# Weights by casting GpSimd DMAs, one staging buffer each for Q, K and V, and the attention's norm in four pieces

## The chip, the cores and the metric

The kernel runs on one core of one Trainium2 chip. The metric is the device time in microseconds (us); lower is better. Executions of one kernel agree to within about 1%. The profile shows one execution: its *span* is the time from its first to its last instruction, and beside it stands the *granted clock* of TensorE, where 1.00 is full speed.

Engines: TensorE (PE) multiplies matrices, VectorE (DVE), ScalarE (ACT) and GpSimd (POOL) do the rest, SyncE (SP) issues transfers. The transfers themselves are made by DMA engines, 16 by the profile's count.

## The reference

Linear attention with an RMS norm, then a two-layer network with ELU.

```python
kv  = einsum('bhsd,bhse->bhde', k, v)             # 8 batches, 8 heads, 576 tokens, head width 64
out = einsum('bhsd,bhde->bhse', q, kv)
rms = sqrt(mean(out * out, axis=-1, keepdims=True) + 1e-6)
a   = out / rms * g_norm
x   = a.transpose(0, 2, 1, 3).reshape(4608, 512)  # 4608 tokens, 512 wide
h   = x @ w_in                                    # 512 x 2048
g   = where(h > 0, h, exp(min(h, 0)) - 1)
y   = g @ w_out                                   # 2048 x 512, float32
```

All inputs are float32. The kernel multiplies in bf16, so every input is cast once.

## The kernel before

The tokens are cut into nine tiles of 512. For each tile there is attention (K'V, transposed Q, their product, the norm, a transposition to x), a *first product* of eight steps (x times w_in, with ELU), and an *output product* (times w_out). Attention for tile T+1 is woven between the steps of tile T's first product, so that TensorE has work while ScalarE and VectorE do the norm and the ELU.

Inputs come through one DMA queue, SyncE's, into a pool of six float32 staging tiles that Q, K, V and the weights share; GpSimd then casts them. (Cuts are marked `# ...`.)

```python
stage = tile_pool(name="stage", bufs=6)
# ...
def fetch_w_out(s):                       # 1 MiB of float32; fetch_w_in is alike
    st = stage_tile()[:, 0:2048]
    nc.sync.dma_start(out=st..., in_=moe_w_out...[:, 4 * s : 4 * s + 4, :])
    raw["wo", s] = st
def cast_w_out(s, eng):
    st = raw.pop(("wo", s))...
    for c in range(KC):
        copy_on(eng, w_out_sb[:, 4 * s + c, :], st[:, c, :])
# ...
def se(h):                                # half a tile of attention's product and its norm
    def run():
        se_ps = at_tile(FP32)...          # PSUM, one buffer
        for c in range(2):
            se_mm(T, 2 * h + c, st["qT"], se_ps[:, c, :])      # TensorE
        ss = sum_heads(square(se_ps, 2), 2)                    # ScalarE, then VectorE
        inv_rms(ss)                                            # ScalarE: Ln, Exp
        # ...
        scale_rows(st["xs"][:, 2 * h : 2 * h + 2, :], se_ps, ss, 2)   # VectorE
    return run
# ...
def mm1(T, i, cols=(slice(0, 512),), relu=False):   # a step of the first product
    # ... 8 matmuls into h_ps (two buffers) ...
    nc.scalar.activation(e, h_ps, AF.Exp)
    # ... with relu=True also a Relu on ScalarE ...
    def rest():                                      # VectorE: min(e,1)-1, then max (or add) into gT
        # ...
    return rest
# ... the order of loads and casts, after tile 0's attention:
for s in range(2): cast_w_in(s, Q)        # fetched right behind tile 0's Q, K and V
fetch(1)                                  # Q, K, V of tile 1
cast_all(1)
for s in range(2, 4): fetch_w_in(s)
for s in range(2, 4): cast_w_in(s, Q)
for s in range(4): fetch_w_out(s); cast_w_out(s, Q)
fetch(2)
at = attention(1)
steps = {2: "q", 3: "kv", 4: "se0", 6: "se1"}
for i in range(8):                        # first product of tile 0
    # ...
    mm1(0, i, cols, relu=(i % 2 == 1))()
    if i in steps: at[steps[i]]()
mm2_half(0, 0); mm2_half(0, 1)            # first output row block of tile 0: needs all of w_out
at["x"]()                                 # transposition of tile 1
mm2_half(0, 2)
cast_all(2); fetch(3)
# ... tile 1 and the later tiles
```

In the traces an instruction that waits holds up those behind it on its engine (ScalarE's Exp stood 2.48 us behind a waiting Ln), and the loads of one DMA queue landed in the order of their issue.

Of the kernel before, what the change touches and what calls it, by code (L numbers as in the profile page):

```python
# [8 lines left out]
FP32 = mybir.dt.float32  # L9
# [7 lines left out]
def kernel(  # L17
# [14 lines left out]
    P = 128  # L32
# [10 lines left out]
    NT = B + 1  # L43

    const = ctx.enter_context(tc.tile_pool(name="const", bufs=1))
    stage = ctx.enter_context(tc.tile_pool(name="stage", bufs=6))
    qkvp = ctx.enter_context(tc.tile_pool(name="qkvp", bufs=2))
    attp = ctx.enter_context(tc.tile_pool(name="attp", bufs=2))
    mlpg = ctx.enter_context(tc.tile_pool(name="mlpg", bufs=2))
# [19 lines left out]
    w_out_sb = const.tile([P, FC, DM], BF16, name="w_out_sb")  # L69


    def stage_tile():
        return stage.tile([P, 2304], FP32, name="st", tag="st")

    raw, bf = {}, {}

    def fetch_q(b):

        st = stage_tile()[:, 0:2048]
        raw["q", b] = st  # L80
        if b < B:
            for s in range(2):
                nc.sync.dma_start(
                    out=st.rearrange("p (s h x) -> p s h x", s=2, h=4)[:, s],
                    in_=q[b].rearrange("(h s) r d -> s h r d", s=2)[s, :, 0:G, :].rearrange(
                        "h (p j) d -> p h (j d)", j=J
                    ),
                )
        else:
            sv = st.rearrange("p (i s h d) -> p i s h d", i=J, s=2, h=4)  # L90
            for t in range(B):
                for s in range(2):
                    nc.sync.dma_start(
                        out=sv[(t % 2) * 64 : (t % 2) * 64 + 64, t // 2, s],
                        in_=q[t].rearrange("(h s) r d -> s h r d", s=2)[
                            s, :, G:S, :
                        ].rearrange("h p d -> p h d"),
                    )

    def fetch_kv(name, src, b):  # L100

        st = stage_tile()
        raw[name, b] = st
        return st.rearrange("p (h x) -> p h x", h=4), src[b].rearrange(
            "h r d -> (h r d)"
        ).rearrange("(h p x) -> p h x", h=4, p=P)
# [4 lines left out]
            out_, in_ = fetch_kv(name, src, b)  # L111
            nc.sync.dma_start(out=out_, in_=in_)

    def fetch_w_in(s):
        st = stage_tile()[:, 0:2048]
        nc.sync.dma_start(
            out=st.rearrange("p (c f) -> p c f", c=KC),
            in_=moe_w_in.rearrange("(c p) f -> p c f", p=P)[:, :, s * 512 : s * 512 + 512],
        )
        raw["wi", s] = st  # L120

    def fetch_w_out(s):
        st = stage_tile()[:, 0:2048]
        nc.sync.dma_start(
            out=st.rearrange("p (c f) -> p c f", c=KC),
            in_=moe_w_out.rearrange("(c p) f -> p c f", p=P)[:, 4 * s : 4 * s + 4, :],
        )
        raw["wo", s] = st

    def copy_on(eng, out_, in_):  # L130
        if eng is nc.scalar:
# [20 lines left out]
    def cast_kv(name, b, eng):  # L152
        sv = kv_tile(name, b)
        for lo, hi in ((0, 2), (2, 4), (4, 6), (6, 8), (8, 9)):
            copy_on(eng, bf[name, b][:, lo:hi], sv[:, lo:hi])

    def cast_w_in(s, eng):
        st = raw.pop(("wi", s)).rearrange("p (c f) -> p c f", c=KC)
        for c in range(KC):
            copy_on(eng, w_in_sb[:, c, s * 512 : s * 512 + 512], st[:, c, :])  # L160

    def cast_w_out(s, eng):
        st = raw.pop(("wo", s)).rearrange("p (c f) -> p c f", c=KC)
        for c in range(KC):
            copy_on(eng, w_out_sb[:, 4 * s + c, :], st[:, c, :])


    xT = {}
# [73 lines left out]
    def attention(T):  # L242
        st = {}

        def kv():
            if T == B:
                return
            kv_ps = at_tile(FP32)
            for u in range(2):
                kv_mm(T, [kv_ps[:, 0:512], kv_ps[:, 512:1024]], u)  # L250
            kv_v = kv_ps.rearrange("p (s x e) -> p s x e", s=2, e=P)[:, :, 0:2, :]
            bd_v = bd_kv[:, T].rearrange("p (s u) e -> p s u e", s=2)
            for l in range(2):
                ls = slice(l * 64, l * 64 + 64)
                nc.scalar.copy(bd_v[ls, :, :, ls], kv_v[ls, :, :, ls])

        def q_t():
            qt_ps = at_tile(BF16).rearrange("p (r t) -> p r t", r=NPAIR)
            for p in range(NPAIR):
                q_t_mm(bf["q", T], qt_ps, p)  # L260
            qT = attp.tile([P, NPAIR, G], BF16, name="qT", tag="qT")
            st["qT"] = qT
            nc.vector.tensor_copy(out=qT[:, 0:2, :], in_=qt_ps[:, 0:2, :])  # L263
            nc.scalar.copy(qT[:, 2:4, :], qt_ps[:, 2:4, :])  # L264

        def se(h):
            def run():
                se_ps = at_tile(FP32).rearrange("p (c f) -> p c f", c=2)
                for c in range(2):
                    se_mm(T, 2 * h + c, st["qT"], se_ps[:, c, :])  # L270
                ss = sum_heads(square(se_ps, 2), 2)
                inv_rms(ss)
                if h == 0:
                    st["xs"] = attp.tile([P, J, DM], BF16, name="xs", tag="xs")
                scale_rows(st["xs"][:, 2 * h : 2 * h + 2, :], se_ps, ss, 2)

            return run

        def x_t():
            xs = st["xs"]  # L280
            xt_ps = at_tile(BF16).rearrange("p (r t) -> p r t", r=NPAIR)
            for c in range(KC):
                for j in range(J):
                    nc.tensor.transpose(  # L284
                        xt_ps[:, c, j * P : j * P + P],
                        xs[:, j, c * P : c * P + P],
                        ident,
                    )
            x = attp.tile([P, KC, G], BF16, name="xT", tag="xT")
            xT[T] = x  # L290
            nc.vector.tensor_scalar(  # L291
                out=x[:, 0:2, :], in0=xt_ps[:, 0:2, :], scalar1=g_col, scalar2=None, op0=ALU.mult
            )
            nc.scalar.mul(x[:, 2:4, :], xt_ps[:, 2:4, :], g_col)  # L294

        return {"kv": kv, "q": q_t, "se0": se(0), "se1": se(1), "x": x_t}


    gT = {}
# [90 lines left out]
    g_src = bass.AP(tensor=g_norm.tensor, offset=g_norm.offset, ap=[[1, 64], [1, 1]])  # L390
    for i in range(2):
        nc.sync.dma_start(out=g_col[i * 64 : i * 64 + 64, :], in_=g_src)
    for s in range(2):
        fetch_w_in(s)

    q_st = q_tile(0)
    qt_ps = ps_m1.tile([P, 2, G], FP32, name="qt_ps", tag="mm1").rearrange(
# [17 lines left out]
    kv_ps = [ps_m2.tile([P, DM], FP32, name="kv_ps", tag="mm2") for _ in range(2)]  # L415
    for u in range(2):
        for n, name in enumerate("kv"):
            for eng, js in ((V, slice(0, 5)), (A, slice(5, 9))):
                copy_on(
                    eng,  # L420
                    bf[name, 0][:, js, 2 * u : 2 * u + 2, :],
                    kv_st[n][:, js, 2 * u : 2 * u + 2, :],
                )
            if (u, n) == (0, 0):
                nc.vector.tensor_copy(out=qT0[:, 0:2, :], in_=qt_ps[:, 0:2, :])
                nc.scalar.copy(qT0[:, 2:4, :], qt_ps[:, 2:4, :])
        kv_mm(0, kv_ps, u)
        if u == 0:
            idle(6)
        for eng, l in ((V, 0), (A, 1)):  # L430
            ls = slice(l * 64, l * 64 + 64)
            for s in range(2):
                copy_on(
                    eng,
                    bd_kv[ls, 0, 2 * s + u, ls],
                    kv_ps[s][ls, u * P + l * 64 : u * P + l * 64 + 64],
                )
# [57 lines left out]
    def cast_all(b):  # L495
        cast_q(b, Q)
        if b < B:
            cast_kv("k", b, Q)
            cast_kv("v", b, Q)

    for s in range(2):
        cast_w_in(s, Q)
    fetch(1)
    cast_all(1)
    for s in range(2, 4):
        fetch_w_in(s)
    for s in range(2, 4):
        cast_w_in(s, Q)
    for s in range(4):
        fetch_w_out(s)  # L510
        cast_w_out(s, Q)
    fetch(2)
    at = attention(1)
    steps = {2: "q", 3: "kv", 4: "se0", 6: "se1"}
    for i in range(8):
        cols = (slice(0, 256), slice(256, 512)) if i == 0 else (slice(0, 512),)
        mm1(0, i, cols, relu=(i % 2 == 1))()
        if i in steps:
            at[steps[i]]()
    mm2_half(0, 0)  # L520
    mm2_half(0, 1)
    at["x"]()
# [2 lines left out]
    cast_all(2)  # L525
    fetch(3)
    at = attention(2)
    halves = {0: 3, 2: 4, 4: 5, 6: 6}
    steps = {1: "q", 2: "kv", 3: "se0", 5: "se1", 7: "x"}
    for i in range(8):  # L530
        rest = mm1(1, i)
        if i in halves:
            mm2_half(0, halves[i])
        rest()
        if i in steps:
            at[steps[i]]()
    mm2_half(0, 7)

    steps = {0: "kv", 1: "q", 2: "se0", 4: "se1", 6: "x"}
    for T in range(2, NT):  # L540
        if T + 1 < NT:
            at = attention(T + 1)
            cast_all(T + 1)
        if T + 2 < B:
            fetch(T + 2)
        elif T + 2 == B:
            fetch_q(B)
        for i in range(8):
            rest = mm1(T, i)
            mm2_half(T - 1, i)  # L550
            rest()
            if T + 1 < NT and i in steps:
                at[steps[i]]()
    for i in range(8):
        mm2_half(NT - 1, i)

# [29 lines left out]
```

## Time and profile before

| | before |
|---|---|
| time, median | 323.12 us (322.09 to 323.97) |
| span of the profiled execution | 320.4 us, granted clock 1.00 |
| first product of tile 0 starts / ends (first output matmul) | 22.0 / 45.5 us |
| transposition of tile 1 / its first product start | 51.95 / 54.57 us |
| one later tile | 31.5 us |

The busy time in windows, kernel before. The columns are the window, its length, busy us and count of instructions of TensorE (PE), its weight loads, VectorE, ScalarE, GpSimd, then the clock, the DMA share and GB/s.

```profile
22.00:30.00 8.00, 6.54 (x53) 4.23 (x52) 3.71 (x5) 3.97 (x4) 6.24 (x11) 1.00 1.05 390
30.00:38.00 8.00, 5.56 (x63) 3.16 (x62) 4.09 (x6) 4.57 (x8) 7.85 (x14) 1.00 1.06 387
38.00:46.00 8.00, 5.74 (x32) 2.71 (x31) 6.75 (x8) 5.02 (x7) 7.58 (x12) 1.00 1.06 373
46.00:54.60 8.60, 5.71 (x39) 2.91 (x39) 5.06 (x6) 3.70 (x6) 7.17 (x14) 1.00 1.06 378
...
151.80:183.30 31.50, 31.29 (x212) 16.10 (x214) 19.22 (x23) 15.84 (x22) 7.90 (x14) 1.00 0.41 143
```

In a later tile (last line) TensorE is busy 31.29 of 31.50 us: nothing is to be won there. Between 22 and 54.6 us it is busy 5.6 to 6.5 of each 8 us, while the DMA engines run at 373 to 390 GB/s without a pause.

The timeline of TensorE, kernel before: start, duration, instruction, count, and in brackets the idle time before it and what ended it. L344 is the output product, L284 the transposition of tile 1, L310 the first product.

```profile
51.51 0.60 PE L344 MATMUL o_ps<-w_out_sb,gT 128*128 128x512 bf16 x2 [2.84 <-DVE gT L328]
51.95 1.06 PE L284 MATMUL at<-ident,xs 128*128 128x128 bf16 x16
...
54.57 1.89 PE L310 MATMUL h_ps<-xT,w_in_sb 128*128 128x512 bf16 x8
```

The last two matmuls of tile 0's first output block waited 2.84 us for the last ELU step (gT).

Waits, kernel before: who waited for whom, total us, times, longest.

```profile
ACT ss L231 <- DVE ss L225: 24.7, 16, 2.5
```

ScalarE stood in its queue before Ln, 16 times, for VectorE's sum; the next Exp of the ELU stood behind it. This wait is what the norm's split aims at.

The timeline of GpSimd, kernel before, the casts of w_out:

```profile
37.39 4.78 POOL L134 CAST w_out_sb<-st 128x512 bf16<-128x512 f32 x8
42.59 5.37 POOL L134 CAST w_out_sb<-st 128x512 bf16<-128x512 f32 x8 [0.42 <-DMA st<-in_moe_w_out_dram]
```

w_out is complete in bf16 at 47.96 us.

### The profile page before, as it was taken

What the parts mean: (1) busy time and instruction counts of PE and PEld (TensorE: products, weight loads), DVE (VectorE), ACT (ScalarE), POOL (GpSimd) and SP (SyncE); (2) the same over time, 40 slices, a digit from 0 to 9 for tenths busy, and PEclk for the clock granted to TensorE, in tenths of its full rate; (3) what the DMA queues carried; (4) which work ended last, traced back from release to release, by engine and by line L of the source; (5) the groups of instructions that cost most, each with busy time, mean ns of one, the idle gap of its engine ahead of it and who ended that gap; (6) DMA issues with size and microseconds to landing.
All of it is one profiled execution on the core that took longest, in us unless ns stands there. A gap on an engine that the chain in (4) does not pass through costs nothing.

```text
span 320.4 us, 4746 instructions
## 1 busy us (share of the span) xinstructions
PE 295.8 (92%) x1905; PEld 149.7 (47%) x1941; DVE 179.2 (56%) x215; ACT 151.8 (47%) x215; POOL 78.4 (24%) x140
## 2 busy tenths in 40 slices
PE   8777686988899999999999999999999999999993
PEld 3443343554454445455545455545454545444441
DVE  3466584558447754775377537744874576454400
ACT  3654654356445544544544455444544545443220
POOL 0069998920026002600260045002000000000000
PEclk9999999999999999999999999999999999999999
DMA  7999999800193019302920392024201010101122
GB/s 255 354 376 389 386 374 376 314 0 2 61 354 119 25 68 349 139 4 89 368 102 2 108 363 88 0 90 99 78 1 65 2 65 2 65 0 65 68 65 65
DMA packets 28565, 46.44 MB, mean 145 GB/s; under 512 B 5504, under 2 KB 13696, under 8 KB 28544
## 3 DMA queue, kind: packets, MB, share of 16 engines
q1 hardware_dynamic: 28544, 46.14, 41.1%
q8 instruction: 15, 0.25, 0.3%
q14 instruction: 6, 0.05, 0.0%
HBM read 36.70 MB, written 9.44 MB: 144 GB/s over the span
## 4 chain that ended last, share of the span: by engine, by line
PE 78%; DMA 7%; DVE 5%; ACT 5%; issue 2%; SPq 1%; POOL 0%; DVEq 0%
PE o_ps L344 36%; PE h_ps L310 33%; DMA st<-in_moe_w_in_dram 5%; DMA st<-in_v_dram 3%; ACT elu_e L318 2%; PE at L179 2%; PE at L284 2%; DVE gT L328 2%; PE at L189 2%; PE at L201 2%; DVE ss L225 1%; DVE elu_e L325 1%; ACT sq L220 1%; DVE xs L235 1%; ACT elu_h L322 1%
## 5 line engine op out<-in xcount | busy, mean ns | idle before, releaser
L310 PE MATMUL h_ps<-xT,w_in_sb 128*128 128x512 bf16 (+1 forms) x564 | 133.8, 376 | 6.3 <-DVE gT L328 3.6
L344 PE MATMUL o_ps<-w_out_sb,gT 128*128 128x512 bf16 x562 | 133.9, 379 | 3.6 <-DVE gT L328 2.8
L318 ACT ACTIVATE elu_e<-h_ps 128x1024 bf16<-128x1024 f32 x72 | 73.5, 1020 | 50.2 <-PE h_ps L310 49.0
L344 PEld LDWEIGHTS <-gT 128*128 128x128 bf16 x576 | 56.2, 98 | 70.6 <-DVE gT L328 3.3
L328 DVE TENSOR_TENSOR gT<-elu_e,h_ps 128x1024 bf16<-128x1024 bf16 x68 | 83.0, 1221 | 7.1
L310 PEld LDWEIGHTS <-w_in_sb 128*128 128x128 bf16 x584 | 55.2, 98 | 65.2 <-issue 3.2
L325 DVE TENSOR_SCALAR elu_e<-elu_e 128x1024 bf16<-128x1024 bf16 x72 | 33.3, 462 | 87.8 <-ACT elu_e L318 87.8
L134 POOL CAST q_bf<-st 128x512 bf16<-128x512 f32 x32 | 18.9, 629 | 125.1 <-DMA st<-in_q_dram 103.4
L354 ACT COPY o_sb<-o_ps 128x512 f32<-128x512 f32 x36 | 21.0, 583 | 24.5 <-PE o_ps L344 24.5
L235 DVE TENSOR_TENSOR xs<-at,ss 128x1024 bf16<-128x1024 f32 x16 | 19.6, 1225 | 9.9 <-ACT ss L232 9.9
L220 ACT ACTIVATE sq<-at 128x1024 bf16<-128x1024 f32 (+1 forms) x18 | 17.5, 977 | 14.5 <-PE at L201 12.0
L225 DVE TENSOR_REDUCE ss<-sq 128x16 f32<-128x1024 bf16 x16 | 19.5, 1218 | 4.8 <-ACT sq L220 4.7
L134 POOL CAST k_bf<-st 128x512 bf16<-128x512 f32 (+1 forms) x35 | 20.1, 617 | 5.3 <-DMA st<-in_k_dram 4.5
L134 POOL CAST v_bf<-st 128x512 bf16<-128x512 f32 (+1 forms) x35 | 18.9, 584 | 0.7
L294 ACT ACTIVATE xT<-at,g_col 128x1024 bf16<-128x1024 bf16 x8 | 8.9, 1114 | 18.5 <-DVE xT L291 18.5
L231 ACT ACTIVATE ss<-ss,eps_col 128x16 f32<-128x16 f32 x16 | 4.9, 307 | 24.7 <-DVE ss L225 24.7
L404 PE MATMUL idle_ps<-zeros,ident 128*128 128x512 bf16 x43 | 13.3, 446 | 1.6 <-POOL ident masks.py:199 1.4
L264 ACT COPY qT<-at 128x1024 bf16<-128x1024 bf16 x8 | 8.1, 1012 | 12.3 <-DVE qT L263 12.3
L134 POOL CAST w_in_sb<-st 128x512 bf16<-128x512 f32 x16 | 9.8, 655 | 15.8 <-DMA st<-in_moe_w_in_dram 15.8
L179 PEld LDWEIGHTS <-k_bf 64*128 64x128 bf16 x288 | 8.2, 94 | 8.7 <-issue 4.1
L179 PE MATMUL at<-v_bf,k_bf 64*128 64x128 bf16 x252 | 8.3, 216 | 3.0 <-POOL w_in_sb L134 2.3
L201 PEld LDWEIGHTS <-qT 128*128 128x128 bf16 x128 | 8.4, 98 | 5.2 <-issue 1.9
(48 smaller groups left out, 117.6 us busy)
## 6 DMA issues: line engine op xcount, KB each, us to landing
st<-in_q_dram SPq DMA_DIRECT2D x16, 512.0 KB, 6.3
out_dram<-o_sb SPq DMA_DIRECT2D x16, 512.0 KB, 3.1
st<-in_k_dram SPq DMA_DIRECT2D x7, 1152.0 KB, 9.4
st<-in_v_dram SPq DMA_DIRECT2D x7, 1152.0 KB, 11.0
st<-in_moe_w_in_dram SPq DMA_DIRECT2D x4, 1024.0 KB, 12.8
st<-in_moe_w_out_dram SPq DMA_DIRECT2D x4, 1024.0 KB, 13.8
st<-in_k_dram SPq DMA_DIRECT2D x2, 576.0 KB, 7.2
st<-in_v_dram SPq DMA_DIRECT2D x2, 576.0 KB, 8.1
```

Source lines behind the costliest of these rows:

```text
L134: eng.tensor_copy(out=out_, in_=in_)
L179: nc.tensor.matmul(kv_ps[s][:, u * P : u * P + P], lhsT=bf["k", T][rows, j, 2 * u : 2 * u + 2, :], rhs=bf["v", T][rows, j, 2 * u : 2 * u + ...
L201: nc.tensor.matmul(ov[:, u, :, s, :], lhsT=qT[:, p, j * P : j * P + P], rhs=bd_kv[:, T, p, :], start=True, stop=True,)
L220: nc.scalar.activation(sq, se_ps, AF.Square)
L225: nc.vector.reduce_sum(out=ss, in_=sq.rearrange("p c (h e) -> p (c h) e", h=H), axis=AX.X)
L235: nc.vector.tensor_tensor(out=xs.rearrange("p c (h e) -> p (c h) e", h=H), in0=se_ps.rearrange("p c (h e) -> p (c h) e", h=H), in1=ss.to_b ...
L310: nc.tensor.matmul(h_ps[:, a, cs], lhsT=w_in_sb[:, c, f * P : f * P + P], rhs=x[:, c, cs], start=(c == 0), stop=(c == KC - 1),)
L318: nc.scalar.activation(e, h_ps, AF.Exp)
L325: nc.vector.tensor_scalar(out=e, in0=e, scalar1=1.0, scalar2=1.0, op0=ALU.min, op1=ALU.subtract)
L328: nc.vector.tensor_tensor(out=gT[T][:, 2 * i : 2 * i + 2, :], in0=e, in1=h, op=ALU.add if relu else ALU.max,)
L344: nc.tensor.matmul(o_ps[T, j], lhsT=gT[T][:, f, j * P : j * P + P], rhs=w_out_sb[:, f, :], start=(f == 0), stop=(f == FC - 1),)
L354: nc.scalar.copy(o_sb[T][:, j % 2, :], o_ps.pop((T, j)))
```

## The change

Its intent: let the DMA cast the weights on the way (float32 in HBM to bf16 in SBUF, issued from GpSimd's queue), so that 32 casts and the weights' staging go away; give Q, K and V one staging buffer each; and put the norm's sum, Ln/Exp and scaling a step of the product later, so that no engine's queue is stopped by them. The first cast of V is split three ways, so that GpSimd starts w_in only when the first half of tile 0's V is there. The core of the diff, condensed (cuts marked with dots):

```diff
-    stage = tile_pool(name="stage", bufs=6)
+    stage = tile_pool(name="stage", bufs=1)           # tags "q", "k", "v"
...
-    def fetch_w_out(s):  ... nc.sync.dma_start(out=st..., in_=moe_w_out...)
-    def cast_w_out(s, eng):  ...
+    def load_w_out(s):
+        fs = slice(4 * s, 4 * s + 4)
+        nc.gpsimd.dma_start(out=w_out_sb[:, fs, :], in_=moe_w_out...[:, fs, :])
...                                                    (w_in alike)
-            def run():  product, square, sum, Ln/Exp, scaling
+            def product(): ...    # and the square
+            def sums(): ...
+            def inv(): ...        # Ln, Exp
+            def scale(): ...
+            return product, sums, inv, scale
...
-    for s in range(2): fetch_w_in(s)                  # behind tile 0's loads, on SyncE's queue
...
+            if (u, n) == (0, 1):
+                parts = ((V, slice(0, 4)), (A, slice(4, 7)), (Q, slice(7, 9)))
...
-    for s in range(2): cast_w_in(s, Q)
-    fetch(1)
-    cast_all(1)
-    for s in range(2, 4): fetch_w_in(s)
-    for s in range(2, 4): cast_w_in(s, Q)
-    for s in range(4): fetch_w_out(s); cast_w_out(s, Q)
-    fetch(2)
+    fetch(1)
+    for s in range(2): load_w_in(s)
+    cast_q(1, Q)
+    for s in range(2, 4): load_w_in(s)
+    cast_kv("k", 1, Q)
+    cast_kv("v", 1, Q)
+    for s in range(4): load_w_out(s)
+    fetch(2)
+    def first_products(T, at, halves, start, relu=()):
+        early, late = {}, {}
+        for name, i in start.items():
+            late.setdefault(i, []).append(name)
+            if name in ("se0", "se1"):
+                early.setdefault(i + 1, []).extend(("sum" + name[2], "inv" + name[2]))
+                late.setdefault(i + 1, []).append("mul" + name[2])
+        for i in range(8):
+            rest = mm1(T, i, cols, relu=i in relu)
+            for name in early.get(i, ()): at[name]()
+            if i in halves: mm2_half(T - 1, halves[i])
+            rest()
+            for name in late.get(i, ()): at[name]()
```

More of the change, by code (lines that the diff above doesn't have):

```diff
@@ L45 @@
     const = ctx.enter_context(tc.tile_pool(name="const", bufs=1))
-    stage = ctx.enter_context(tc.tile_pool(name="stage", bufs=6))
+    stage = ctx.enter_context(tc.tile_pool(name="stage", bufs=1))
     qkvp = ctx.enter_context(tc.tile_pool(name="qkvp", bufs=2))
@@ L69, with stage_tile @@
     w_out_sb = const.tile([P, FC, DM], BF16, name="w_out_sb")
-    def stage_tile():
-        return stage.tile([P, 2304], FP32, name="st", tag="st")
+    def stage_tile(tag):
+        return stage.tile([P, 2304], FP32, name=f"st_{tag}", tag=tag)
     raw, bf = {}, {}
     def fetch_q(b):
-        st = stage_tile()[:, 0:2048]
+        st = stage_tile("q")[:, 0:2048]
         raw["q", b] = st
@@ L100, in fetch_kv @@
     def fetch_kv(name, src, b):
-        st = stage_tile()
+        st = stage_tile(name)
         raw[name, b] = st
@@ L112, in fetch, with load_w_in @@
             nc.sync.dma_start(out=out_, in_=in_)
-    def fetch_w_in(s):
-        st = stage_tile()[:, 0:2048]
-        nc.sync.dma_start(
-            out=st.rearrange("p (c f) -> p c f", c=KC),
-            in_=moe_w_in.rearrange("(c p) f -> p c f", p=P)[:, :, s * 512 : s * 512 + 512],
-        )
-        raw["wi", s] = st
-    def fetch_w_out(s):
-        st = stage_tile()[:, 0:2048]
-        nc.sync.dma_start(
-            out=st.rearrange("p (c f) -> p c f", c=KC),
-            in_=moe_w_out.rearrange("(c p) f -> p c f", p=P)[:, 4 * s : 4 * s + 4, :],
+    def load_w_in(s):
+        cols = slice(s * 512, s * 512 + 512)
+        nc.gpsimd.dma_start(
+            out=w_in_sb[:, :, cols], in_=moe_w_in.rearrange("(c p) f -> p c f", p=P)[:, :, cols]
+        )
+    def load_w_out(s):
+        fs = slice(4 * s, 4 * s + 4)
+        nc.gpsimd.dma_start(
+            out=w_out_sb[:, fs, :], in_=moe_w_out.rearrange("(c p) f -> p c f", p=P)[:, fs, :]
         )
-        raw["wo", s] = st
     def copy_on(eng, out_, in_):
@@ L155, in cast_kv @@
             copy_on(eng, bf[name, b][:, lo:hi], sv[:, lo:hi])
-    def cast_w_in(s, eng):
-        st = raw.pop(("wi", s)).rearrange("p (c f) -> p c f", c=KC)
-        for c in range(KC):
-            copy_on(eng, w_in_sb[:, c, s * 512 : s * 512 + 512], st[:, c, :])
-    def cast_w_out(s, eng):
-        st = raw.pop(("wo", s)).rearrange("p (c f) -> p c f", c=KC)
-        for c in range(KC):
-            copy_on(eng, w_out_sb[:, 4 * s + c, :], st[:, c, :])
     xT = {}
@@ L266, in se, with product @@
         def se(h):
-            def run():
+            def product():
                 se_ps = at_tile(FP32).rearrange("p (c f) -> p c f", c=2)
@@ L270, in run, with sums, inv, scale @@
                     se_mm(T, 2 * h + c, st["qT"], se_ps[:, c, :])
-                ss = sum_heads(square(se_ps, 2), 2)
-                inv_rms(ss)
+                st["se", h] = se_ps
+                st["sq", h] = square(se_ps, 2)
+            def sums():
+                st["ss", h] = sum_heads(st.pop(("sq", h)), 2)
+            def inv():
+                inv_rms(st["ss", h])
+            def scale():
                 if h == 0:
                     st["xs"] = attp.tile([P, J, DM], BF16, name="xs", tag="xs")
-                scale_rows(st["xs"][:, 2 * h : 2 * h + 2, :], se_ps, ss, 2)
-            return run
+                rows = st["xs"][:, 2 * h : 2 * h + 2, :]
+                scale_rows(rows, st.pop(("se", h)), st.pop(("ss", h)), 2)
+            return product, sums, inv, scale
         def x_t():
@@ L294, in x_t @@
             nc.scalar.mul(x[:, 2:4, :], xt_ps[:, 2:4, :], g_col)
-        return {"kv": kv, "q": q_t, "se0": se(0), "se1": se(1), "x": x_t}
+        pieces = {"kv": kv, "q": q_t, "x": x_t}
+        for h in range(2):
+            for name, piece in zip(("se", "sum", "inv", "mul"), se(h)):
+                pieces[f"{name}{h}"] = piece
+        return pieces
     gT = {}
@@ L392 @@
         nc.sync.dma_start(out=g_col[i * 64 : i * 64 + 64, :], in_=g_src)
-    for s in range(2):
-        fetch_w_in(s)
     q_st = q_tile(0)
@@ L417 @@
         for n, name in enumerate("kv"):
-            for eng, js in ((V, slice(0, 5)), (A, slice(5, 9))):
+            parts = ((V, slice(0, 5)), (A, slice(5, 9)))
+            if (u, n) == (0, 1):
+                parts = ((V, slice(0, 4)), (A, slice(4, 7)), (Q, slice(7, 9)))
+            for eng, js in parts:
                 copy_on(
@@ L499, in cast_all @@
             cast_kv("v", b, Q)
+    fetch(1)
     for s in range(2):
-        cast_w_in(s, Q)
-    fetch(1)
-    cast_all(1)
+        load_w_in(s)
+    cast_q(1, Q)
     for s in range(2, 4):
-        fetch_w_in(s)
-    for s in range(2, 4):
-        cast_w_in(s, Q)
+        load_w_in(s)
+    cast_kv("k", 1, Q)
+    cast_kv("v", 1, Q)
     for s in range(4):
-        fetch_w_out(s)
-        cast_w_out(s, Q)
+        load_w_out(s)
     fetch(2)
-    at = attention(1)
-    steps = {2: "q", 3: "kv", 4: "se0", 6: "se1"}
-    for i in range(8):
-        cols = (slice(0, 256), slice(256, 512)) if i == 0 else (slice(0, 512),)
-        mm1(0, i, cols, relu=(i % 2 == 1))()
-        if i in steps:
-            at[steps[i]]()
+    def first_products(T, at, halves, start, relu=()):
[6 more added lines that the diff above has]
+        for i in range(8):
+            cols = (slice(0, 256), slice(256, 512)) if T == 0 and i == 0 else (slice(0, 512),)
+            rest = mm1(T, i, cols, relu=i in relu)
+            for name in early.get(i, ()):
+                at[name]()
+            if i in halves:
+                mm2_half(T - 1, halves[i])
+            rest()
+            for name in late.get(i, ()):
+                at[name]()
+    at = attention(1)
+    first_products(0, at, {}, {"q": 2, "kv": 3, "se0": 4, "se1": 6}, (1, 3, 5, 7))
     mm2_half(0, 0)
@@ L527 @@
     at = attention(2)
-    halves = {0: 3, 2: 4, 4: 5, 6: 6}
-    steps = {1: "q", 2: "kv", 3: "se0", 5: "se1", 7: "x"}
-    for i in range(8):
-        rest = mm1(1, i)
-        if i in halves:
-            mm2_half(0, halves[i])
-        rest()
-        if i in steps:
-            at[steps[i]]()
+    first_products(
+        1, at, {0: 3, 2: 4, 4: 5, 6: 6}, {"q": 1, "kv": 2, "se0": 3, "se1": 5, "x": 7}
+    )
     mm2_half(0, 7)
-    steps = {0: "kv", 1: "q", 2: "se0", 4: "se1", 6: "x"}
+    halves = {i: i for i in range(8)}
     for T in range(2, NT):
+        at, start = None, {}
         if T + 1 < NT:
-            at = attention(T + 1)
+            at, start = attention(T + 1), {"kv": 0, "q": 1, "se0": 2, "se1": 4, "x": 6}
             cast_all(T + 1)
@@ L547 @@
             fetch_q(B)
-        for i in range(8):
-            rest = mm1(T, i)
-            mm2_half(T - 1, i)
-            rest()
-            if T + 1 < NT and i in steps:
-                at[steps[i]]()
+        first_products(T, at, halves, start)
     for i in range(8):
```

## The prediction

> **What bounds the kernel now.** Three stretches. From about 55 us to the end TensorE is the limit: in the busy-by-window view, 151.8 to 183.3 us is one token tile of 31.5 us with TensorE busy 31.29, VectorE 19.2 and ScalarE 15.8, granted clock 1.00 throughout. The waits by engine show only some 3 us of TensorE waits after 56 us. The start, 0 to 22 us, ends with the first transposed tile; its chain is DMA (the second half of V lands at 12.46 us), casts, norm. Between, 22 to 54.6 us, TensorE is busy only 5.5 to 6.5 us of each 8, while DMA is saturated (373 to 390 GB/s in every window from 8 to 54 us).
>
> The idle there, from the timeline of TensorE: 1.41 us on the ELU's last VectorE step, 2.28 before the K'V product (really ScalarE's copy of qT, ending at 33.71), 1.17 and 1.09 around the norm, 2.84 at 48.6 to 51.5 on the last ELU tile; 9 us with the small ones. ScalarE stands 2.48 and 2.19 us in its queue before Ln, waiting for VectorE's sum, and the next Exp waits behind it; VectorE then waits 0.62 for Ln/Exp before the scaling.
>
> **What the change does.**
> 1. Norm in pieces: the sum comes a step later, and Ln/Exp after that step's Exp. This removes the two head-of-queue stops of 2.2 to 2.5 us. VectorE's own work in the first product is about 8 x 1.6 + 5.5 = 18.3 us (estimate from the durations of the trace) against 23.5 us spent now (22.0 to 45.5); the tail after it (6 us to the second half product's last matmuls) should fall to about 3.5. Worth 4 to 6 us if data are there. Nothing in the later tiles, which TensorE fills already.
> 2. Weights cast in flight: 32 casts, about 20 us of GpSimd, vanish, and the tensor_scalar that ran 0.66 to 0.88 us beside GpSimd's casts (0.42 alone) get a little faster. Bytes read from HBM stay the same, so no DMA time is saved.
> 3. Order of DMA: before, one queue served w_in, Q/K/V of tile 1, w_in, w_out, then tile 2. After, Q/K/V of tiles 1, 2 and partly 3 run on their own queue beside the weights[...]. w_out is issued only after tile 1's casts, at about 28 to 32 us. Before, 15.2 MB went ahead of w_out's end: at 378 GB/s plus 2.5 us of ramp, about 43 us. After, some 18.6 to 19.5 MB, so estimate 48 to 54 us, while its last use would otherwise come at 45 to 46. The gain of step 1 is thus largely taken back by a wait for w_out. The first w_in transfers may also share bandwidth with the end of V and delay the start by 0 to 1.5 us.
>
> **Predicted:** 320.5 us (before 323.12), range 315 to 327. Chances: faster by over 2% 0.18, within 2% 0.70, slower 0.12.
>
> **What would show it.** ScalarE's waits for VectorE's sum nearly gone, and the first product shorter than 21 us; a TensorE wait for a DMA of w_out before the first output tile's second half; later tiles still 31.5 us; DMA still near 378 GB/s to about 60 us.
>
> **What would make it wrong.** If the GpSimd queue gets more than half of the engines, w_out comes earlier (nearer 315) but V later. If the cast slows DMA[...], w_in itself comes late and the time rises past 327. If my estimate of the step time is off, VectorE still bounds the first product and little moves.

15.2 MB at 378 GB/s plus 2.5 us of ramp made about 43 us for the kernel before, and the same sum gives 51.7 to 54.1 us for 18.6 to 19.5 MB, put down as 48 to 54. That both queues share that one rate was an assumption of mine, and so was the delay of the start by w_in's first loads. A ramp of that size shows in the trace of the kernel before: 0, 7 and 125 GB/s in the first three us, 385 in the fourth. That trace's windows show 361 GB/s from 8 to 22 us, and 373 to 390 only from 22 us on.

## The result, and the profile after

Ratios here and below are the mean time of one kernel's fast runs over that of the kernel before in the same rounds, so not quite the ratio of the medians quoted.

| | before | after |
|---|---|---|
| time, median | 323.12 us | 330.89 us (330.57 to 331.73) |
| ratio | | 1.0246 (95%: 1.021 to 1.0281) |
| span, mean clock | 320.4, 1.00 | 329.9, 0.975 |
| first product of tile 0 starts / ends | 22.0 / 45.5 | 21.7 / 45.7 |
| transposition of tile 1 starts | 51.95 | 60.21 |
| first product of tile 1 starts | 54.57 | 64.66 |
| last run of output matmuls starts | 299.4 | 308.8 |

The two profiled executions lie further apart than the medians (spans 9.5 us, medians 7.8): the changed kernel's is the slowest of its four, and that of the kernel before ran at full clock.

So the loss is made between 46 and 65 us; what follows takes as long as before (the K'V products of two later tiles start at 98.08 and 129.60 us after, at 88.64 and 120.17 before: 31.5 us both times).

Windows, changed kernel, columns as above:

```profile
38.00:46.00 8.00, 5.52 (x32) 2.60 (x31) 7.61 (x9) 5.58 (x9) 4.60 (x8) 1.00 1.13 288
46.00:54.00 8.00, 2.30 (x9) 0.84 (x9) 2.88 (x4) 2.24 (x4) 2.63 (x5) 0.77 1.17 251
54.00:62.00 8.00, 4.71 (x24) 2.64 (x23) 0.00 (x0) 0.59 (x1) 4.05 (x8) 0.50 0.97 323
62.00:70.00 8.00, 7.95 (x36) 3.48 (x35) 2.40 (x3) 2.72 (x3) 3.50 (x7) 0.88 0.04 15
```

TensorE is busy 2.30 of the 8 us from 46 to 54, and the mean clock of the windows falls to 0.77, then 0.50. (In finer windows the clock is seen to stand at 0.50 from 50.32 to 63.97 us and at 1.00 on both sides.) The GB/s count what was *written*: a casting transfer writes half of what it reads. (The whole kernel wrote 42.24 MB by this count, 46.44 before; the difference of 4.2 MB is just half of the weights' 8.4 MB.)

Timeline of TensorE, changed kernel. L345 is the output product, L281 the transposition of tile 1, L311 the first product; the three lines with "<-DMA" are the stops.

```profile
45.69 1.03 PE L345 MATMUL o_ps<-w_out_sb,gT 128*128 128x512 bf16 x3
49.10 1.02 PE L345 MATMUL o_ps<-w_out_sb,gT 128*128 128x512 bf16 x4 [2.38 <-DMA w_out_sb<-in_moe_w_out_dram]
53.39 1.86 PE L345 MATMUL o_ps<-w_out_sb,gT 128*128 128x512 bf16 x4 [3.27 <-DMA w_out_sb<-in_moe_w_out_dram]
58.55 1.86 PE L345 MATMUL o_ps<-w_out_sb,gT 128*128 128x512 bf16 x4 [3.29 <-DMA w_out_sb<-in_moe_w_out_dram]
60.21 1.91 PE L281 MATMUL at<-ident,xs 128*128 128x128 bf16 x16
61.91 2.91 PE L345 MATMUL o_ps<-w_out_sb,gT 128*128 128x512 bf16 x8
64.66 1.89 PE L311 MATMUL h_ps<-xT,w_in_sb 128*128 128x512 bf16 x8
```

Three of the four pieces of w_out are waited for; the last comes at 58.5 us. Behind it, four matmuls take 1.86 us where they took 1.02 after the first stop, and eight take 2.91 where they take 1.89 later: the clock is halved, until it rises again at 63.97 us, within these eight.

Waits, changed kernel:

```profile
PE o_ps L345 <- DMA w_out_sb<-in_moe_w_out_dram: 8.9, 3, 3.3
...
PE h_ps L311 <- DMA w_in_sb<-in_moe_w_in_dram: 2.1, 1, 2.1
...
ACT ss L217 <- DVE ss L211: 0.8, 1, 0.8
```

ScalarE's wait for the sum is gone (24.7 to 0.8 us), as intended. The waits for weights are new.

The timeline of SyncE's queue, changed kernel (K, V of tile 2; Q, K, V of tile 3; first store), and the issue of w_out on GpSimd's queue:

```profile
27.30 0.37 SPq L112 DMA_DIRECT2D st_k<-in_k_dram  x1
32.81 0.37 SPq L112 DMA_DIRECT2D st_v<-in_v_dram  x1
39.80 0.92 SPq L83 DMA_DIRECT2D st_q<-in_q_dram  x2
45.56 0.37 SPq L112 DMA_DIRECT2D st_k<-in_k_dram  x1
51.10 0.37 SPq L112 DMA_DIRECT2D st_v<-in_v_dram  x1
68.93 0.36 SPq L364 DMA_DIRECT2D out_dram<-o_sb  x1
```

```profile
L122 POOL DMA_DIRECT2D w_out_sb<-in_moe_w_out_dram x4: 745/765/777, 32.7 to 34.9; - x4
...
DMA to landing us min/median/max: 11.5/17.4/23.6
```

w_out was issued from 32.7 us (the last piece at 34.9), and took up to 23.6 us. In that time the other queue, which no longer stands behind the weights, loaded K and V of tile 2 and most of tile 3. Up to 58.5 us the profile counts 287 GB/s x 58.5 us = 16.8 MB written; with 4.2 MB more read than written, 21.0 MB of source data. Over 56 us (the 2.5 us of ramp left out) that is 375 GB/s, the rate of before.

### The profile page after: what moved, and what is told of

It is laid out like the page before. It is cut to its first block, busy times and chain, and to the rows that moved or that the text cites. A ratio compares the mean times of both kernels' runs of the same rounds, so it can differ in the third digit from the quotient of the medians.

```text
span 329.9 us, 4698 instructions
## 1 busy us (share of the span) xinstructions
PE 299.3 (91%) x1905; PEld 151.0 (46%) x1941; DVE 178.3 (54%) x215; ACT 153.5 (47%) x215; POOL 65.2 (20%) x117
## 2 busy tenths in 40 slices
DMA packets 28565, 42.24 MB, mean 128 GB/s; under 512 B 5504, under 2 KB 17792, under 8 KB 28544
## 3 DMA queue, kind: packets, MB, share of 16 engines
HBM read 36.70 MB, written 9.44 MB: 140 GB/s over the span
## 4 chain that ended last, share of the span: by engine, by line
PE 78%; DMA 12%; DVE 3%; ACT 3%; POOL 1%; issue 1%; DVEq 0%; POOLq 0%; SPq 0%
PE o_ps L345 36%; PE h_ps L311 32%; DMA w_out_sb<-in_moe_w_out_dram 7%; DMA st_v<-in_v_dram 5%; PE at L281 2%; PE at L165 2%; PE idle_ps L403 2%; PE at L175 2%; PE at L187 2%; DVE gT L329 1%; ACT elu_e L319 1%; POOL v_bf L130 1%; DVE elu_e L326 1%; POOL w_out_sb L122 0%; DVE xs L221 0%
## 5 line engine op out<-in xcount | busy, mean ns | idle before, releaser
L345 PE MATMUL o_ps<-w_out_sb,gT 128*128 128x512 bf16 x561 | 137.0, 385 | 9.8 <-DMA w_out_sb<-in_moe_w_out_dram 8.9
L311 PE MATMUL h_ps<-xT,w_in_sb 128*128 128x512 bf16 (+1 forms) x565 | 133.9, 376 | 5.0 <-DMA w_in_sb<-in_moe_w_in_dram 2.1
L345 PEld LDWEIGHTS <-gT 128*128 128x128 bf16 x576 | 56.8, 99 | 78.7 <-issue 12.7
L311 PEld LDWEIGHTS <-w_in_sb 128*128 128x128 bf16 x584 | 55.1, 98 | 63.7 <-DMA w_in_sb<-in_moe_w_in_dram 2.6
L130 POOL CAST q_bf<-st_q 128x512 bf16<-128x512 f32 x32 | 18.9, 628 | 144.2 <-DMA st_q<-in_q_dram 144.2
L130 POOL CAST v_bf<-st_v 128x512 bf16<-128x512 f32 (+1 forms) x36 | 20.1, 601 | 14.4 <-DMA st_v<-in_v_dram 14.1
L130 POOL CAST k_bf<-st_k 128x512 bf16<-128x512 f32 (+1 forms) x35 | 19.6, 602 | 12.0 <-DMA st_k<-in_k_dram 12.0
L211 DVE TENSOR_REDUCE ss<-sq 128x16 f32<-128x1024 bf16 x16 | 19.5, 1218 | 4.1 <-ACT sq L206 4.0
L221 DVE TENSOR_TENSOR xs<-at,ss 128x1024 bf16<-128x1024 f32 x16 | 19.5, 1217 | 0.0
L288 DVE TENSOR_SCALAR xT<-at,g_col 128x1024 bf16<-128x1024 bf16 x8 | 6.0, 745 | 12.5 <-PE at L281 12.5
L187 PE MATMUL at<-bd_kv,qT 128*128 128x128 bf16 x120 | 9.1, 219 | 2.7 <-DVE xs L221 2.7
```

What stands on the lines that cost most here:

```text
L130: eng.tensor_copy(out=out_, in_=in_)
L187: nc.tensor.matmul(ov[:, u, :, s, :], lhsT=qT[:, p, j * P : j * P + P], rhs=bd_kv[:, T, p, :], start=True, stop=True,)
L211: nc.vector.reduce_sum(out=ss, in_=sq.rearrange("p c (h e) -> p (c h) e", h=H), axis=AX.X)
L221: nc.vector.tensor_tensor(out=xs.rearrange("p c (h e) -> p (c h) e", h=H), in0=se_ps.rearrange("p c (h e) -> p (c h) e", h=H), in1=ss.to_b ...
L311: nc.tensor.matmul(h_ps[:, a, cs], lhsT=w_in_sb[:, c, f * P : f * P + P], rhs=x[:, c, cs], start=(c == 0), stop=(c == KC - 1),)
L345: nc.tensor.matmul(o_ps[T, j], lhsT=gT[T][:, f, j * P : j * P + P], rhs=w_out_sb[:, f, :], start=(f == 0), stop=(f == FC - 1),)
```

## The experiments

The theory (T in the expectations): w_out is late because tiles 2 and 3 are loaded at the same time over the same DMA engines, and the halved clock adds to it. Rivals: the norm's split costs (R3); the cast in flight, or its issue from GpSimd, is slow in itself (R2); GpSimd's queue issues w_out too late (R1); the single staging buffers throttle the loads (R4). All kernels gave correct results. "Before" in the table is the kernel before in the same rounds.

| run | median us | before | ratio (95%) | last piece of w_out lands, us |
|---|---|---|---|---|
| the changed kernel, 4 runs | 330.89 | 323.12 | 1.0246 (1.021 to 1.0281) | 58.5 |
| after_again | 331.54 | 323.15 | 1.0251 (1.0222 to 1.0279) | 58.4 |
| a_norm_undone | 331.54 | 323.45 | 1.0239 (1.0213 to 1.0265) | 58.4 |
| b_norm_only | 319.97 | 323.45 | 0.9896 (0.9866 to 0.9925) | (staged, as before) |
| c_hold_2_3 | 322.73 | 323.45 | 0.9975 (0.9911 to 1.0038) | 47.4 |
| c2_hold_3 | 326.16 | 323.45 | 1.0078 (1.0049 to 1.0107) | 54.0 |
| d_fill | 329.34 | 322.66 | 1.0203 (1.0148 to 1.0257) | 58.9 |
| d_fill_again | 330.58 | 323.15 | 1.0216 (1.0178 to 1.0254) | 58.0 |
| e_early_issue | 329.73 | 322.66 | 1.0202 (1.015 to 1.0254) | 57.0 |
| f_two_buffers | 330.84 | 322.66 | 1.0225 (1.0174 to 1.0277) | 57.1 |
| g_in_order_of_need | 323.10 | 322.66 | 0.9987 (0.9936 to 1.0038) | 50.8 |
| h_hold_fill | 321.94 | 323.15 | 0.9958 (0.9931 to 0.9986) | 47.6 |
| i_hold_fill_early | 320.46 | 323.16 | 0.9931 (0.9897 to 0.9965) | 44.5 |

The landing is the start of the last piece's first matmul where TensorE waited for it, else the last issue plus the longest time to landing.

### The norm's split, taken out of the changed kernel, and put alone into the kernel before

```diff
 a_norm_undone, against the changed kernel
-                early.setdefault(i + 1, []).extend(("sum" + name[2], "inv" + name[2]))
-                late.setdefault(i + 1, []).append("mul" + name[2])
+                late[i].extend(("sum" + name[2], "inv" + name[2], "mul" + name[2]))
 b_norm_only, against the kernel before: the four pieces and first_products(); loads, casts, staging untouched
```

> The changed kernel with the norm's four pieces put back in one place (sum, Ln/Exp and scaling right after the product). Theory T (the last three pieces of w_out arrive late because tiles 2 and 3 are loaded over the same DMA engines at the same time): the first output tile waits for w_out until about 58.5 us whatever the norm does, so the time is that of the changed kernel, 329 to 332.5 us, and the gap of TensorE shortens as the product ends later. Rival R3 (the split of the norm itself costs the time): back to about 323 us.

> The kernel before with only the norm split; weights, queue and staging as before. Theory T: no late w_out (its last cast ends at about 48 us), later tiles at 31.5 us; the first output tile no longer waits until 51.5, so 319 to 322.5 us, ratio 0.988 to 0.998. Rival R3 (the split costs): 326 us or more.

Both came as theory T had it, 331.54 and 319.97 us. The split is worth 1% alone (0.9896) and nothing that shows in the changed kernel (ratio 1.0239 without it, 1.0246 with it), where the transposition of tile 1 waits for w_out until 60 us with the split (60.21) and without it (60.05). Timeline of TensorE, b_norm_only (here L359 is the output product, L295 the transposition, L325 the first product):

```profile
45.82 3.62 PE L359 MATMUL o_ps<-w_out_sb,gT 128*128 128x512 bf16 x16
49.88 1.05 PE L295 MATMUL at<-ident,xs 128*128 128x128 bf16 x16 [0.43 <-DVE xs L235]
...
52.49 1.89 PE L325 MATMUL h_ps<-xT,w_in_sb 128*128 128x512 bf16 x8
```

The sixteen output matmuls run through without a stop, and tile 1 is 2.1 us ahead of the kernel before. The first product itself is not shorter (21.65 to 45.82 us): VectorE was busy 7.69 of the 8 us from 38 to 46 in that run. The gain lies in what follows it.

### Tiles 2 and 3 held back until w_out has landed

```diff
 c_hold_2_3 (c2_hold_3: the same two lines before fetch(3) instead)
+    probe = const.tile([1, 16], BF16, name="probe")
+    nc.sync.dma_start(out=probe, in_=w_out_sb[0:1, FC - 1, 0:16])   # SyncE's queue waits here for w_out
     fetch(2)
```

> The changed kernel, but a 32-byte copy out of the last piece of w_out stands in the load queue ahead of tile 2's Q, K and V, so tiles 2 and 3 are fetched after w_out. Theory T: 15.2 MB of source data ahead of w_out's end at about 372 GB/s plus 2.5 us, so w_out lands at 43.5 to 46 us, TensorE's waits for it fall from 8.9 to under 1.5 us, the clock stays at 1.00, and the time is 318.5 to 323.5 us. Rival R2 (casting in flight[...] are slow in themselves): w_out still lands after 52 us and the time stays above 327 us.

> The same copy, but ahead of tile 3 only, so tile 2 still shares the DMA with w_out. Theory T: 18.6 MB ahead of w_out's end, so about 52.5 us (50.5 to 54.5), half way between the other two, and 323.5 to 328 us. R2: no change from 331 us.

Timeline of TensorE, c_hold_2_3:

```profile
35.14 1.80 PE L165 MATMUL at<-v_bf,k_bf 64*128 64x128 bf16 x36 [2.24 <-ACT qT L250]
...
48.23 3.62 PE L345 MATMUL o_ps<-w_out_sb,gT 128*128 128x512 bf16 x15
52.28 1.05 PE L281 MATMUL at<-ident,xs 128*128 128x128 bf16 x16 [0.43 <-DVE xs L221]
```

Timeline of TensorE, c2_hold_3:

```profile
51.50 1.02 PE L345 MATMUL o_ps<-w_out_sb,gT 128*128 128x512 bf16 x4 [1.42 <-DMA w_out_sb<-in_moe_w_out_dram]
54.02 1.02 PE L345 MATMUL o_ps<-w_out_sb,gT 128*128 128x512 bf16 x4 [1.50 <-DMA w_out_sb<-in_moe_w_out_dram]
54.88 1.06 PE L281 MATMUL at<-ident,xs 128*128 128x128 bf16 x16
```

With both tiles held, no output matmul waits for w_out; with tile 3 alone held, the last piece comes at 54.0 us; with none held, at 58.5. The times follow, 322.73, 326.16 and 330.89 us. This is a dose and its response, and it shows the cause: the loads of tiles 2 and 3 beside w_out. c_hold_2_3 landed w_out 1.4 us later than the expected 46, because GpSimd issued it only at 32 us and the weights' queue had run dry before (129 GB/s in all from 30 to 38 us); nothing waited for it. Its clock did not stay at 1.00 as expected: it was 0.986 in the profiled run, halved for 3.4 us from 11.62 and from 35.52 us.

That the cast is not slow is seen where it has the DMA to itself. Window of c_hold_2_3 in which only w_out moved:

```profile
40.00:46.00 6.00, 3.83 (x20) 1.61 (x18) 4.93 (x7) 5.12 (x7) 0.00 (x0) 1.00 1.14 189
```

189 GB/s written are at most 378 GB/s of float32 read (372 without the instruction loads that the 189 include), about as much as plain loads reached in the kernel before (377 from 8 to 62 us). R2 falls.

### Earlier issue; two staging buffers

```diff
 e_early_issue
     for s in range(2, 4): load_w_in(s)
+    for s in range(4): load_w_out(s)
     cast_kv("k", 1, Q)
     cast_kv("v", 1, Q)
-    for s in range(4): load_w_out(s)
 f_two_buffers
-    stage = tile_pool(name="stage", bufs=1)
+    stage = tile_pool(name="stage", bufs=2)
```

> The changed kernel with w_out's four loads issued on GpSimd's queue before the casts of K and V of tile 1 (at about 21 instead of 33 us). Theory T: the queue of the weights was never empty before 33 us (w_in's last piece was still under way), so an earlier issue moves nothing; w_out ends at 57 to 60 us, 329 to 332.5 us. Rival R1 (GpSimd's queue in order issues w_out too late): w_out ends 7 us or more earlier, 325 us or less.

> The changed kernel with two staging buffers each for Q, K and V. Theory T: both queues were loaded all the time already, so no gain; the loads of tiles 2 and 3 run further ahead and w_out ends at 58 to 61 us: 330 to 333.5 us. Rival R4 (one buffer each makes the loads wait for the casts, and that delays everything): 328 us or less.

w_out, e_early_issue: form, count, duration, first and last issue; then the time to landing.

```profile
L122 POOL DMA_DIRECT2D w_out_sb<-in_moe_w_out_dram x4: 760/775/787, 21.1 to 23.3; - x4
...
DMA to landing us min/median/max: 21.5/28.3/33.7
```

Issued 12 us earlier (the last piece at 23.3 instead of 34.9), w_out took 33.7 us instead of 23.6 and landed at 57.0: 1.5 us gained of 12. R1 falls as the main cause. Two buffers brought w_out at 57.1 us, a little before the 58 to 61 expected, and 330.84 us: R4 falls.

### The clock

```diff
 d_fill, d_fill_again (the same kernel)
-    mm2_half(0, 1)
+    fill(13)              # matmuls of zeros into an unused PSUM tile
+    mm2(0, 0, 8, 12)
+    fill(17)
+    mm2(0, 0, 12, 16)
```

> The changed kernel with 13 and 17 matmuls of zeros, results unused, put into TensorE's waits for the third and fourth piece of w_out (about 2.8 and 3.7 us of the 3.3 and 4.2 us of idle time). The granted clock of the changed kernel was 0.77 in 46 to 54 us and 0.50 in 54 to 62. Theory T with the clock as its second term: w_out comes at the same 58.5 us, but the clock stays near 1.00, so the transposes and output products after it take about 1.06 and 1.9 us instead of 1.91 and 2.91; 3 us less, 327 to 329.5 us. If the clock is not a cause: 330 to 332 us.

> The changed kernel unaltered, as the partner of the next run on the same chip. 329 to 332 us, mean clock 0.97 to 0.985; ratio to before 1.021 to 1.028.

> The fill of TensorE's waits once more, now beside the changed kernel itself. In the trace of the first try the stretch from w_out's arrival to the next tile's first product took 3.5 us against 6.1. If that is the clock's whole share: 1.5 to 2.7 us below after_again. If the fill brought nothing: within 0.7 us of it.

Timeline of TensorE, d_fill, to be held against the lines from 58.55 us of the changed kernel:

```profile
59.20 1.03 PE L345 MATMUL o_ps<-w_out_sb,gT 128*128 128x512 bf16 x4
...
62.68 1.89 PE L311 MATMUL h_ps<-xT,w_in_sb 128*128 128x512 bf16 x8
```

From the arrival of w_out to the first product of tile 1 it takes 3.48 us (59.20 to 62.68) instead of 6.11 (58.55 to 64.66). So in this stretch the halved clock costs 2.6 us. In the whole time less is seen, and nothing clear of the noise: 329.34 us at first, inside the range expected, but with an interval that overlaps the changed kernel's; then 330.58 beside after_again's 331.54, which is 1.0 us and not the 1.5 to 2.7 expected, and the intervals overlap again. The fill runs' clock also fell elsewhere: their times lie at 328.9 to 329.8 us where the mean clock was 0.991 or more, and at 331.5 to 331.9 where it was 0.989 or less. That the clock halves and slows what follows is shown; how much of the 7.8 us it is, from nothing clear of the noise up to 2.6, stays open (the second pair gives 1.0).

When did the clock fall? In the changed kernel at 50.32 us, only 0.2 us after the first stop of 3.27 us had begun (50.12). So the length of that stop did not bring the fall. Before it, from 46.90 to 50.32 us, TensorE was busy 1.02 us, with the stop of 2.38 us in it. In the traces of the two kernels the clock's record starts at 5.95 us (changed kernel) and 6.28 us (before) at 1.00, and the changes lie at 50.32, 63.97 and 326.80 us, and at 320.30 us: 13, 4 and 77, and 92 times 3.41 us apart. Of the steps of 3.41 us counted so (up to 295 us, busy shares worked out from the two packed traces; some matmul records may be missing), those at full clock with less than half of TensorE's time busy are three: the one from 46.90 us in the changed kernel, with 30%, after which the clock fell, and those from 30.17 and 47.23 us in the kernel before, with 41 and 42%, after which it did not. In other executions of the kernel before the mean clock was 0.994 or 0.989, so there it did fall.

What a fall goes with in the whole time is seen in eleven executions of the kernel before in one set of rounds: 322.1 to 322.5 us at a mean clock of 0.998 or 0.999, 323.1 to 323.2 at 0.994, 324.2 to 324.5 at 0.988 to 0.990. A step of 3.41 us at half clock lowers the mean by 0.005 (estimate: 1.7 of 321 us), so one step went with about 1 us.

### The loads in the order of need, and a version that mends

```diff
 g_in_order_of_need: c_hold_2_3, and
-    fetch(1)
+    fetch_q(1)
     for s in range(2): load_w_in(s)
+    nc.sync.dma_start(out=probe_in, in_=w_in_sb[0:1, KC - 1, 1008:1024])
+    ... fetch K and V of tile 1 ...
     cast_q(1, Q)
+    cast_kv("k", 1, Q)
     for s in range(2, 4): load_w_in(s)
-    cast_kv("k", 1, Q)
     cast_kv("v", 1, Q)
 h_hold_fill: c_hold_2_3, and
-        idle(2)
+        idle(2 if s == 0 else 7)          # zeros before the first K'V product
+                if T == 0 and name == "kv":   ... 9 matmuls of zeros ...
 i_hold_fill_early: h_hold_fill, and w_out issued before the casts of K and V of tile 1
```

> The changed kernel with all loads in the order of need: tiles 2 and 3 held until w_out has landed, K and V of tile 1 held until w_in's second piece has landed, w_in's third and fourth piece issued after K's cast. Theory T: the 1.8 to 2.1 us wait for w_in's second piece goes as well as that for w_out (which lands at 44 to 48 us); 317.5 to 321.5 us, below the kernel before and about equal to the norm's split alone. If the order of loads is not what costs, no better than 322.7 us, the run that held tiles 2 and 3 only.

g_in_order_of_need missed its range, 323.10 us, and w_out landed at 50.8 us instead of 44 to 48. The wait for w_in went, but K and V of tile 1, held until 22.7 us, came late in turn: TensorE waited 4.3 us for V's casts before tile 1's K'V product. I had held too hard; the run exchanged one wait for another.

> The run that held tiles 2 and 3 until w_out had landed, with 5 more matmuls of zeros before the first K'V product and 9 in the wait before tile 1's. Theory: what that run (322.7 us, mean clock 0.986) still lacks against the norm's split alone (320.0 us, clock 0.997) is the clock that drops after TensorE's pauses at 9 and 33 us; with them filled the clock is 0.995 or more and the time 319.5 to 321.5 us. Rival: it is the cast in flight itself, or the wait for w_in (1.8 us); then it stays at 322 us or more.

h_hold_fill, 321.94 us at a clock of 0.999 in the profiled run, fell between the two expectations. Timeline of TensorE, h_hold_fill:

```profile
52.05 1.89 PE L311 MATMUL h_ps<-xT,w_in_sb 128*128 128x512 bf16 x8
...
62.44 0.29 PE L165 MATMUL at<-v_bf,k_bf 64*128 64x128 bf16 x4 [0.70 <-POOL v_bf L130]
```

At 52.05 us it was ahead of b_norm_only (52.49). It lost that at 62 us, where K'V of tile 2 stopped for V's casts: tile 2 had been held for too long.

> The held and filled run, with w_out issued on GpSimd's queue before the casts of K and V of tile 1. In the held and filled run the weights' queue stood empty for a time before w_out's issue at 32.7 us, w_out landed at 47.5, and tile 2's V came so late that its K'V product (62.4 us) stopped for casts; at 52.1 us it had still been 0.4 us ahead of the norm's split alone. Theory: with tiles 2 and 3 held, an earlier issue does count: w_out lands at 43.5 to 46 us, tile 2 is fetched 2 to 3 us earlier, the stop at 62 us goes, and the time is 318.5 to 321 us, ratio 0.985 to 0.993. If an earlier issue brings nothing here either, as it did while tiles 2 and 3 were loaded beside it: 321.5 us or more.

Here the earlier issue counts. Window of i_hold_fill_early while weights alone were loaded (the end of tile 1's V landed at 30.4 us), then its TensorE timeline:

```profile
30.00:39.00 9.00, 8.59 (x84) 4.80 (x83) 3.97 (x6) 5.66 (x8) 2.83 (x5) 1.00 1.24 207
```

```profile
52.59 1.89 PE L311 MATMUL h_ps<-xT,w_in_sb 128*128 128x512 bf16 x8
...
62.86 1.18 PE L165 MATMUL at<-v_bf,k_bf 64*128 64x128 bf16 x36 [0.59 <-ACT qT L250]
```

w_out landed at 44.5 us, the stop at 62 us went, and the time was 320.46 us, 0.7% below the kernel before, and its interval overlaps that of b_norm_only. The same 12 us of earlier issue that brought 1.5 us of earlier landing in e_early_issue brought 3.1 us here (47.6 to 44.5). 207 GB/s written are at most 414 GB/s of source (411 without the instruction loads): by then the casting transfers, alone, ran faster than the two queues together.

So there are versions that beat both kernels, by about 1% or less: the norm's split alone, which is the simplest and has the lowest time, and the whole change with the loads held and the weights issued early. In these runs casting in flight added nothing to what the norm's split brings: the 20 us of GpSimd's casts that it saves were not on the critical path (GpSimd had 0% of the kernel before's chain). No run casts in flight without the split and with the loads held, so its worth alone is not shown.

## Why the prediction was wrong

The prediction was 320.5 us (315 to 327) and the time was 330.89.

1. *"Later tiles still 31.5 us", "nothing in the later tiles".* Right: 31.5 us before and after.
2. *"ScalarE's waits for VectorE's sum nearly gone."* Right: 24.7 to 0.8 us. *"The first product shorter than 21 us"*: wrong. It took 24.0 us, of which 2.1 were the wait for w_in's second piece, and 24.2 in b_norm_only without that wait. VectorE still fills 38 to 46 us. The split's gain came in the tail: 4.1 us instead of 6.5 from the first output matmul to the transposition. Alone it is worth 3.5 us of the 4 to 6 predicted.
3. *"Bytes read stay the same, so no DMA time is saved."* Right: 36.70 MB were read from HBM before and after, at 375 GB/s of source data after, against 377.
4. *"After, some 18.6 to 19.5 MB, so estimate 48 to 54 us."* This is the step that failed. The mechanism was the right one, and so was the rate; the term that was mis-sized is the bytes ahead of w_out's end. It was 21.0 MB, and w_out landed at 58.5 us. I had counted tile 2 and part of tile 3's Q; in fact Q and nearly all of K of tile 3 came too. The queue of the activations stops only where its program stops: before the first store (68.93 us), which waits for the output that waits for w_out. Until then it goes on to tile 3 as fast as GpSimd frees the staging buffers. With 21.0 MB the prediction's own sum (378 GB/s and 2.5 us) gives 58.1 us. For 18.6 MB it gives 51.7; c2_hold_3, in which just these went ahead, landed at 54.0. So tile 3's bytes make 4.5 us of the miss, and about 2 us are in the sum itself (in which of its terms is not shown). The step from the landing to the time was too mild as well: c2_hold_3 has w_out at the upper end of the estimate, 54 us, and took 326.16 us, 2.7 more than the kernel before in its rounds, where the prediction had 2.6 less.
5. *The clock* is missing from the prediction. A wait of TensorE was costed as its length; but the work behind the last stop ran at half speed, for 2.6 us more in that stretch (of which the whole time shows about 1, not clear of the noise). Short stops stood before a fall: 2.38 us in the changed kernel (half clock from 50.32 us, after four more matmuls at full speed), and 2.24 us in c_hold_2_3 (half clock from 35.52 us), where the K'V product at 35.14 us took 1.80 us instead of the 1.18 at full clock. Stops of 2.28 and 2.84 us in the kernel before did not bring one in the profiled run (1.00 until 320.30 us).
6. *"May delay the start by 0 to 1.5 us."* In the profiled run the first product began 0.3 us earlier (21.7 for 22.0 us); in c_hold_2_3, which starts in the same way, 0.9 us later (22.9), with the clock at one half from 11.62 to 15.04 us.
7. *"If the GpSimd queue gets more than half of the engines."* It did not. The weights' 8.4 MB took from 9.8 to 58.5 us, 172 GB/s, 46% of 375. The one rate for both queues, assumed in the prediction, agrees with what was measured: 375 GB/s of source for both together, 377 for the one queue before.

Shown: that w_out is late because of the loads beside it (c, c2, i), that the norm's split is good alone and hidden here (a, b), that neither the cast's rate, nor the issue, nor the buffers is the main cause (c, e, f). Left open: the clock's share, and what the cast in flight is worth alone.

## What to carry to other kernels

The second DMA queue added no bandwidth here (375 GB/s against 377); it took away the order that one queue had imposed. Before moving loads to another queue, list what must have landed by when, add up *all* bytes that either queue can issue until then, up to the point where a queue's program itself stops, and hold back what is not needed yet with a dependency. And after a stop of TensorE of 2 us or more look at the granted clock: the stop can cost more than its length (2.6 us more here, in that stretch).
